# A fused attention and mixture-of-experts kernel: the router's normalisation moved from GpSimd to VectorE, and the third token group's operands made without GpSimd

## The chip, the core and the metric

The kernel runs on one core of a Trainium2 chip. The time is the device time of one execution in microseconds. The engines are TensorE (PE; PEld is its weight load), VectorE (DVE), ScalarE (ACT), GpSimd (POOL) and SyncE (SP), whose queue issues nearly all DMAs.

## What is computed

Linear attention, then a gated feed-forward layer, then a mixture of eight experts with a soft router, on 2304 tokens of width 512. The last part is the one that the change touches:

```python
logits = x @ w_gate
logits = logits - logits.max()
P = np.exp(logits)
for _ in range(8):
    P /= P.sum(1, keepdims=True) + 1e-09
    P /= P.sum(0, keepdims=True) + 1e-09
    P *= N / E
out = np.zeros((N, D), dtype=np.float32)
for e in range(E):
    h = np.maximum(x @ w1[e], 0.0)
    ye = h @ w2[e]
    out += P[:, e:e + 1] * ye
```

Here x has 2304 x 512 elements, E is 8, w1[e] is 512 x 1024 and w2[e] is 1024 x 512.

## The kernel before

Everything is float32, split into a high part in TensorE's reduced format (fp32r) and a low part that is the rest; a product is three matmuls (high x high, low x high, high x low). The order of instructions on each engine is the order in which the program writes them, so a step that stands earlier in the program holds up everything behind it on its engine.

The expert stage works through three token groups of 768 tokens (`GROUPS`), each through 8 experts in 4 units of 256 hidden columns: 32 units (`PER`) per group, numbered 0 to 95. The matrix products use Strassen's scheme: seven products of quarter matrices, M1 to M7. Their right-hand sides are the quarters B11, B12, B21, B22 of x and the sums T1 to T4 of them (T1 = B12 - B11, T2 = B22 - T1, T3 = B22 - B12, T4 = B21 - T2), 2 x 384 columns each. `operands` (from L1107) makes these for a group: `summed` makes a T, `high` copies the high part on ScalarE, `low` subtracts for the low part. It is a generator that does one step of a list per call; in the list, T1 is a sum, hT1 its high part, lT1 its low part, and a G in a step puts it on GpSimd instead of VectorE. Each operand gets a tile of the pool `xs`, which has 8 places.

Units 0 to 31 also prepare the experts' weights: `prep_first` and `prep_second` split a unit's weights into high and low parts (L1042 to L1089 on VectorE), some instructions per call of `prep_tick`, and store them to DRAM (`kept`), from where the units of the later groups read them (`recall`). In such a unit `m2_burst` (L1260) writes the products M2, M6, M5, M7, M4, M3 and calls `mid(k)` between them; the first product of the next unit (`m2_m1`) and four of the six second-layer blocks (`m2_s2`) follow. On VectorE the line L1265 adds two products into `cs` and so frees a PSUM bank, L1211 makes the low half of the hidden layer in `hw` and `hq`.

The router's probabilities, 128 partitions x 18 tiles x 8 experts in the tile `probs`, are normalised by the generator `sinkhorn` (from L919). Its steps are put between the work of units 0 to 6 by `next(steps)`: at `mid(4)` and behind the second-layer blocks 0 and 2 of each unit. First comes the maximum over everything, with GpSimd's `partition_all_reduce` (L924). Then in each of eight iterations GpSimd adds the eight columns in three halving steps (`plus`, L931), VectorE takes the reciprocal `rs` (L942), GpSimd multiplies (`times`, L932), adds the 18 tiles in five steps, sums over the partitions (L950) and scales (L951), VectorE takes the reciprocal `ca` (L955), and GpSimd multiplies again.

In groups 1 and 2 (units 32 to 95) a unit is `m2_p1`, the seven first-layer products of unit n, and `m2_p2`, the second layer of unit n - 1; `work(k)` is called at places in both. L1379 adds two products (`add`), L1335 applies relu and the token's probability (`half_mul`), L1349 makes a low part, L1353 a sum for the second layer, L1446 (`m2_fold`) folds a second-layer product from PSUM into `acc`. The probabilities come back as rows spread over all partitions, by `probs_in`, alternating between two places, `pb_place`. The last unit of a group has a plain second layer, `m2_plain`, whose 18 adds are L1486.

The third group's operands are made in a list `ORDER2` of 18 steps: T1 and T2 from units 62 and 63 on, all sums and the low parts of all T on GpSimd, the rest in units 63 and 64. The tiles `fx` and `fy` hold B11 and B22, B21 and B12 of the hidden layer; `fy` takes the place of `accx`, the output of group 0's last two tiles.

## Time and profile before

| | before |
|---|---|
| median of 3 runs | 2132.41 us (2132.09 to 2135.24) |
| the profiled execution | 2136.45 us |
| its span | 2134.6 us, granted TensorE clock 0.975 on average |
| PE busy | 2009.7 us (94%) |
| DVE busy | 1576.8 us (74%) |
| ACT busy | 804.8 us (38%) |
| POOL busy | 201.3 us (9%) |
| chain that ended last | PE 84%, issue 6%, DVE 4%, POOL 2% |

The profile comes from one execution; its times count from the span's start. The span is what the profiler records; the execution's own time lies 1.85 us above it. Group 0 of the expert stage runs from about 560 to 1175 us, group 1 to about 1653, group 2 to the end. Where an engine is idle, the profile names what ended the wait; "issue" means that nothing it shows did.

### The profile page before, as it was taken

To read this page: it belongs to the slowest core of one execution; us is meant where nothing else is said; L and a number is where in the kernel's file an instruction comes from. 1 tells how busy PE (TensorE), PEld (TensorE's weight loads), DVE (VectorE), ACT (ScalarE), POOL (GpSimd) and SP (SyncE) were. 2 spreads that over 40 slices of the span, in tenths; PEclk is the share of its full clock that TensorE was granted. 3 is DMA by queue.
4 is the path that set the end of the run, shared out by engine and by line. 5 is a ranking of instruction groups with operands and counts; after the bars stand their busy time and mean duration, and the time that the engine had idled before them with its cause. 6 is when DMAs were issued, how large, how long until landed. Compare 5 with 4: busy or idle time off the path is not lost.

```text
span 2134.6 us, 29119 instructions
## 1 busy us (share of the span) xinstructions
PE 2009.7 (94%) x10837; PEld 1867.6 (87%) x10837; DVE 1576.8 (74%) x3107; ACT 804.8 (38%) x1594; POOL 201.3 (9%) x274
## 2 busy tenths in 40 slices
PE   8999999999955569999999999999998999999999
PEld 7788888888844458889998999999998999999999
DVE  7865752535633347877777899999999899999998
ACT  5644531323423235545444333333333333333332
POOL 3532211111112210000000000000003000000000
PEclk9999999999977779999999999999999999999999
DMA  8400320100442448778787777776675777667673
GB/s 258 126 23 24 110 65 1 50 35 1 166 154 106 160 177 311 295 292 301 285 315 301 274 261 253 267 261 252 255 269 198 269 259 257 268 257 253 255 265 119
DMA packets 135493, 429.54 MB, mean 201 GB/s; under 512 B 11816, under 2 KB 68024, under 8 KB 135352
## 3 DMA queue, kind: packets, MB, share of 16 engines
q1 hardware_dynamic: 135080, 427.56, 55.4%
q8 instruction: 85, 1.39, 0.3%
q14 instruction: 56, 0.46, 0.1%
q10 hardware_dynamic: 272, 0.13, 0.0%
HBM read 306.20 MB, written 121.45 MB: 200 GB/s over the span
## 4 chain that ended last, share of the span: by engine, by line
PE 84%; issue 6%; DVE 4%; POOL 2%; ACT 1%; DMA 1%; POOLq 0%; ACTq 0%; DVEq 0%
PE sb L1190 30%; PE sb L1431 12%; PE yb L1431 9%; PE yb L1224 3%; PE yb L1225 3%; PE yb L1223 3%; PE pg L801 2%; PE pv L801 2%; PE y L803 2%; PE pg L802 2%; PE pg L803 2%; PE pv L803 2%; PE pv L802 2%; PE y L802 2%; PE y L801 2%
## 5 line engine op out<-in xcount | busy, mean ns | idle before, releaser
L1446 DVE TENSOR_TENSOR acc<-sb,acc 128x384 f32<-128x384 f32 x480 | 260.8, 558 | 27.0 <-PE sb L1431 23.0
L1190 PE MATMUL sb<-op0T,u 128*128 128x384 f32 x768 | 160.2, 353 | 78.6 <-DVE cs L1265 78.6
L1190 PEld LDWEIGHTS sb<-op0T,u 128*128 128x128 f32 x768 | 145.2, 201 | 86.6 <-DVE cs L1265 81.6
L1190 PE MATMUL sb<-op1T,u 128*128 128x384 f32 x768 | 143.9, 335 | 3.3 <-DVE fx L1379 3.3
L1190 PE MATMUL sb<-op2T,u 128*128 128x384 f32 x768 | 144.7, 336 | 0.8 <-ACT mt L1383 0.5
L1190 PEld LDWEIGHTS sb<-op1T,u 128*128 128x128 f32 x768 | 134.0, 188 | 3.9 <-DVE fx L1379 3.9
L1190 PEld LDWEIGHTS sb<-op2T,u 128*128 128x128 f32 x768 | 133.9, 188 | 2.4 <-DVE fx L1379 1.6
L834 DVE SCALAR_TENSOR_TENSOR th<-th,pg 128x512 f32<-128x512 f32 (+1 forms) x60 | 37.9, 632 | 131.4 <-ACT th L833 131.2
L1190 PE MATMUL sb<-op2B,u 128*128 128x384 f32 x576 | 110.8, 335 | 2.7 <-issue 1.7
L1190 PE MATMUL sb<-op1B,u 128*128 128x384 f32 x576 | 110.5, 335 | 2.4 <-DVE fy L1379 2.2
L1190 PE MATMUL sb<-op0B,u 128*128 128x384 f32 x576 | 111.5, 337 | 0.5 <-ACT pT L1311 0.5
L1379 DVE TENSOR_TENSOR fx<-mt,sb 128x384 f32<-128x384 f32 x128 | 70.9, 554 | 54.4 <-ACT mt L1383 42.3
L1431 PE MATMUL sb<-hc,u 128*128 128x384 f32 x504 | 104.4, 335 | 2.2 <-DVE acc L1446 2.2
L841 POOL TENSOR_TENSOR h<-th,h 128x512 fp32r<-128x512 f32 (+1 forms) x60 | 73.2, 1220 | 339.3 <-ACT h L840 339.3
L1190 PEld LDWEIGHTS sb<-op0B,u 128*128 128x128 f32 x576 | 101.5, 188 | 3.4 <-ACT pT L1311 0.8
L1190 PEld LDWEIGHTS sb<-op2B,u 128*128 128x128 f32 x576 | 100.7, 188 | 3.3 <-issue 2.0
L1190 PEld LDWEIGHTS sb<-op1B,u 128*128 128x128 f32 x576 | 100.6, 188 | 3.2 <-DVE fy L1379 2.6
L1431 PE MATMUL sb<-hd,u 128*128 128x384 f32 x492 | 101.7, 334 | 0.0
L1431 PE MATMUL yb<-hd,u 128*128 128x384 f32 x426 | 96.7, 334 | 0.0
L801 PE MATMUL pg<-x,w 128*128 128x512 f32 (+1 forms) x240 | 90.4, 377 | 1.3 <-ACT x L591 1.3
L803 PE MATMUL y<-h,w 128*128 128x512 f32 (+1 forms) x240 | 89.1, 371 | 2.1 <-POOL w L371 2.1
L1431 PEld LDWEIGHTS sb<-hc,u 128*128 128x128 f32 x504 | 88.8, 188 | 2.5 <-DVE acc L1446 2.5
(330 smaller groups left out, 4915.7 us busy)
## 6 DMA issues: line engine op xcount, KB each, us to landing
u<-kept SPq DMA_DIRECT2D x252, 896.0 KB, 6.2
kept<-u SPq DMA_DIRECT2D x64, 896.0 KB, 5.5
kept<-u SPq DMA_DIRECT2D x62, 768.0 KB, 4.4
rw<-in_moe_w_dram SPq DMA_DIRECT2D x64, 512.0 KB, 5.8
kept<-u SPq DMA_DIRECT2D x62, 128.0 KB, 3.9
raw<-in_moe_w_gate_dram SPq DMA_DIRECT2D x10, 512.0 KB, 3.6
...
```

Source lines behind the costliest of these rows:

```text
L801: nc.tensor.matmul(o, lhsT=w(0), rhs=xb[0], start=first, stop=False)
L802: nc.tensor.matmul(o, lhsT=w(0), rhs=xb[1], start=False, stop=False)
L803: nc.tensor.matmul(o, lhsT=w(1), rhs=xb[0], start=False, stop=last)
L834: nc.vector.scalar_tensor_tensor(out=th[:, 0:n], in0=th[:, 0:n], scalar=1.0, in1=pg[:, 0:n], op0=ALU.add, op1=ALU.mult)
L841: nc.gpsimd.tensor_tensor(out=h[:, 1, 0:n], in0=th[:, 0:n], in1=h[:, 0, 0:n].bitcast(F32), op=ALU.subtract)
L1190: nc.tensor.matmul(bank[:, 0:NT], lhsT=w[wz][:, WI[wname], c, :], rhs=x[:, xz, c, :], start=(start and c == 0 and j == 0), stop=(c == 1 an ...
L1223: nc.tensor.matmul(py, lhsT=h[:, 0, s], rhs=w2[0][:, d], start=(u == 0 and f == 0), stop=False)
L1224: nc.tensor.matmul(py, lhsT=h[:, 0, s], rhs=w2[1][:, d], start=False, stop=False)
L1225: nc.tensor.matmul(py, lhsT=h[:, 1, s], rhs=w2[0][:, d], start=False, stop=(u == UE - 1 and f == 1))
L1379: add = lambda o, a, b: nc.vector.tensor_tensor(out=o, in0=a, in1=b, op=ALU.add)
L1431: nc.tensor.matmul(bank[:, 0:NT], lhsT=w[wz][:, d], rhs=h[:, hz], start=(start and k == 0), stop=True, skip_group_check=True)
L1446: nc.vector.tensor_tensor(out=a, in0=bank[:, 0:NT], in1=a, op=ALU.add)
```

## The change

`sinkhorn` now does its arithmetic on VectorE, three pieces per iteration with a yield ahead of each: sum over the experts, EPS, reciprocal; multiply, sum over the tiles, and GpSimd's `partition_all_reduce`; EPS, reciprocal, and one instruction that multiplies by N/E and by the reciprocals. The steps are also taken at `mid(0)`, so four per unit instead of three. GpSimd keeps the partition sums alone.

`ORDER2` has no G any more. Its first seven steps (T1, hT1, lT1, T2, hT2, lT2, T4) are done in units 40 to 46, one in each, at the end of `m2_p2`; the others in units 63 and 64. No tile of `xs` is taken for group 2: T1 and T2 lie in eight strips of 384 columns at the ends of the tiles of group 1's operands and of `hb`, in two parts of one chunk each, so that `high` and `low` take twice as many instructions for them; the other five operands take the tiles of group 1's operands that are no longer read. The second place of `probs_in` is now the old place of `fy` (tile `pb1`), and `fy` the one in `acc[1]` where the odd probabilities were.

```diff
-        room = tp.tile([P, 512], F32, tag="th", name="room")
...
-        plus = lambda o, x, y: nc.gpsimd.tensor_tensor(out=o, in0=x, in1=y, op=ALU.add)
-        times = lambda w: nc.gpsimd.tensor_tensor(out=probs, in0=probs, in1=w, op=ALU.mult)
         for i in range(ITERS):
-            if i == 0:
-                yield
-            plus(h, probs[:, :, 0:4], probs[:, :, 4:8])
-            plus(h[:, :, 0:2], h[:, :, 0:2], h[:, :, 2:4])
+            yield
             rs = mp.tile([P, NTILE], F32, tag="rs", name=f"rs{i}")
-            plus(rs, h[:, :, 0], h[:, :, 1])
-            nc.gpsimd.tensor_scalar(out=rs, in0=rs, scalar1=EPS, scalar2=None, op0=ALU.add)
+            nc.vector.tensor_reduce(out=rs, in_=probs, axis=AX.X, op=ALU.add)
+            nc.vector.tensor_scalar(out=rs, in0=rs, scalar1=EPS, scalar2=None, op0=ALU.add)
+            nc.vector.reciprocal(out=rs, in_=rs)
             yield
-            nc.vector.reciprocal(out=rs, in_=rs)
-            times(rs.unsqueeze(2).to_broadcast([P, NTILE, E]))
-            plus(c, probs[:, 0:9], probs[:, 9:18])
...
+            nc.vector.tensor_tensor(
+                out=probs, in0=probs, in1=rs.unsqueeze(2).to_broadcast([P, NTILE, E]), op=ALU.mult
+            )
+            cs = mp.tile([P, E], F32, tag="cs", name=f"cs{i}")
+            nc.vector.tensor_reduce(out=cs, in_=probs.rearrange("p t e -> p e t"), axis=AX.X, op=ALU.add)
             ca = mp.tile([P, E], F32, tag="ca", name=f"ca{i}")
-            nc.gpsimd.partition_all_reduce(ca, c[:, 0], P, bass_isa.ReduceOp.add)
-            nc.gpsimd.tensor_scalar(
-                out=ca, in0=ca, scalar1=EPS, scalar2=float(E) / N, op0=ALU.add, op1=ALU.mult
+            nc.gpsimd.partition_all_reduce(ca, cs, P, bass_isa.ReduceOp.add)
+            yield
+            nc.vector.tensor_scalar(out=ca, in0=ca, scalar1=EPS, scalar2=None, op0=ALU.add)
+            nc.vector.reciprocal(out=ca, in_=ca)
+            nc.vector.scalar_tensor_tensor(
+                out=probs,
...
-                if k == 4:
+                if k in (0, 4):
                     next(steps, None)
...
-            pb_place = [halves, [flat[1][:, z * NT : (z + 1) * NT] for z in (3, 4)]]
+            pb_place.append(halves)
...
-    fy = xp.tile([P, 1024], F32, tag="xt0", name="fy")
+    pb1 = xp.tile([P, 1024], F32, tag="xt0", name="pb1")
+    pb_place.append([pb1[:, z * NT : (z + 1) * NT] for z in range(2)])
+    fy = flat[1][:, 3 * NT : 5 * NT]
...
-    ORDER2 = ["TG1", "hT1", "lT1G", "TG2", "hB11", "hT2", "lT2G", "TG4", "lB11", "hB21", "hT4", "lT4G", "TG3"]
-    ORDER2 += ["lB21", "hB22", "hT3", "lT3G", "lB22"]
+    for name, old in (("B11", "B11"), ("B21", "B21"), ("T4", "T2"), ("T3", "T1"), ("B22", "T3")):
+        homes[name] = halves_of(tiles[1, old])
+    room = [t[:, 4 * NT : 5 * NT] for t in [tiles[1, name] for name in IN_RING] + [hb_tile]]
+    for k, name in enumerate(("T1", "T2")):
+        homes[name] = None, [[room[4 * k + 2 * z + c] for c in range(2)] for z in range(2)]
+    ORDER2 = ["T1", "hT1", "lT1", "T2", "hT2", "lT2", "T4", "hB11", "hB21", "hT4", "lB11", "lB21", "hB22", "lT4", "T3"]
+    ORDER2 += ["hT3", "lB22", "lT3"]
...
-        if g == 1 and n % PER == PER - 2:
-            until("TG1")
         if start and g > 1:
-            m2_plain(n - 1, lambda k: until(("hB22", "hB22", "lT3G", "lB22")[k]) if k != 1 else None)
-            m2_p1(n, idle)
+            m2_plain(n - 1, at_k("hB22", None, "lT4", "T3"))
+            m2_p1(n, at_k("hT3", "lB22", None, "lT3"))
...
         elif plain(n) and g == 1:
-            m2_p1(n, lambda k: until("TG2") if k == 1 else None)
-            m2_p2(n - 1, lambda k: until(("hB11", "lB11", "hB21", "lB21")[k]))
+            m2_p1(n, at_k(None, "hB11", "hB21", "hT4"))
+            m2_p2(n - 1, at_k(None, "lB11", None, "lB21"))
         else:
             m2_p1(n, idle, (2, 1, 3, 3) if n == PER + 1 else (2, 1, 0, 2))
-            m2_p2(n - 1, idle)
+            pre = n - PER - 8
+            m2_p2(n - 1, at_k(None, None, None, ORDER2[pre]) if g == 1 and 0 <= pre < 7 else idle)
```

The order on the engines shows three places. The first is GpSimd in the normalisation, from the end of one iteration's tile sums to the next multiplication before the change (an ISA row with tiles is a `partition_all_reduce`; one without tiles stands alone):

```order
L931 TENSOR_TENSOR room<-room 128x8 x2
L950 ISA
L950 ISA ca_5016<-room 128x8
L951 ISA
L951 TENSOR_SCALAR ca_5016<-ca_5016 128x8
L932 TENSOR_TENSOR probs<-probs,ca_5016 128x144
```

and with the change, from the maximum on:

```order
L924 ISA
L924 ISA gma<-gm 128x1
L941 ISA ca_4980<-cs_4978 128x8
L941 ISA ca_5068<-cs_5066 128x8
L941 ISA ca_5202<-cs_5200 128x8
```

The rows without tiles at each sum and behind it are gone; the five other sums follow in the same way, and nothing of GpSimd's stands behind the eighth.

The second is VectorE at the end of unit 3, where the normalisation's fourth iteration is; before the change the unit's end holds one reciprocal between pieces of weight preparation (`t`, `u`; `rw` is the loaded weight):

```order
L1211 SCALAR_TENSOR_TENSOR hw<-cs,hw 128x384
L1056 TENSOR_TENSOR u_0_1_5400<-s_5401,u_0_0_5399 128x512
L1058 TENSOR_TENSOR u_0_1_5400<-s_5401,u_0_0_5399 128x512
L1076 TENSOR_TENSOR t_5487<-rw_1_5283 128x256
L1077 TENSOR_TENSOR t_5487<-t_5487,rw_1_5283 128x256
L1080 TENSOR_TENSOR t_5487<-rw_1_5283 128x256
L1081 TENSOR_TENSOR t_5487<-rw_1_5283,t_5487 128x256
L955 RECIPROCAL ca_5460<-ca_5460 128x8
```

and with the change:

```order
L1227 SCALAR_TENSOR_TENSOR hw<-cs,hw 128x384
L1080 TENSOR_TENSOR u_1_1_5268<-rw_1_5116,u_1_0_5267 128x1024
L1083 TENSOR_TENSOR u_1_1_5268<-t_5266,u_1_0_5267 128x512
L1085 TENSOR_TENSOR u_1_1_5268<-t_5266,u_1_0_5267 128x512
L935 TENSOR_TENSOR probs<-probs,rs_5288 128x144
L939 TENSOR_REDUCE cs_5327<-probs 128x8
L943 TENSOR_SCALAR ca_5329<-ca_5329 128x8
L944 RECIPROCAL ca_5329<-ca_5329 128x8
L945 SCALAR_TENSOR_TENSOR probs<-probs,ca_5329 128x144
L931 TENSOR_REDUCE rs_5364<-probs 128x18
L932 TENSOR_SCALAR rs_5364<-rs_5364 128x18
L1281 TENSOR_TENSOR cs<-mc_5310,sb_4675 128x384
```

The third piece of the iteration (L943) now stands directly behind the second (L939), with nothing between, and ahead of the next unit's first `cs`.

The third is VectorE at the beginning of group 2, from the last adds of `m2_plain` to the first add into `fx`; before:

```order
L1486 TENSOR_TENSOR acc_106<-yb_4827,acc_106 128x384
L1140 TENSOR_TENSOR op2B_13515<-acc_108,op2B_13515 128x2x256
L1140 TENSOR_TENSOR op2B_13515<-acc_108,op2B_13515 128x2x128
L1486 TENSOR_TENSOR acc_105<-yb_4824,acc_105 128x384
L1486 TENSOR_TENSOR acc_105<-yb_4825,acc_105 128x384
L1379 TENSOR_TENSOR fx<-mt_9395,sb_4674 128x384
```

and with the change:

```order
L1150 TENSOR_TENSOR op1T_9276<-acc_107,op1T_9276 128x2x256
L1150 TENSOR_TENSOR op1T_9276<-acc_107,op1T_9276 128x2x128
L1502 TENSOR_TENSOR acc_106<-yb_4827,acc_106 128x384
L1163 TENSOR_TENSOR acc_107<-acc_108 128x2x256
L1163 TENSOR_TENSOR acc_107<-acc_108 128x256
L1502 TENSOR_TENSOR acc_105<-yb_4824,acc_105 128x384
L1502 TENSOR_TENSOR acc_105<-yb_4825,acc_105 128x384
L1150 TENSOR_TENSOR op1T_9302<-acc_108,op1T_9302 128x2x256
L1150 TENSOR_TENSOR op1T_9302<-acc_108,op1T_9302 128x2x128
L1395 TENSOR_TENSOR fx<-mt_9354,sb_4674 128x384
```

lT4 (the first two rows) and T3 (L1163) have come into VectorE's list, and lB22 has moved behind the last two adds, directly ahead of the add into `fx`.

## Rows read from the trace of the kernel before

**Rows 1.** Stretches: us, PE, PEld, DVE, ACT, POOL (x count), PEclk, DMA share, GB/s.

```profile
589.71:793.13 203.42, 111.49 (x470) 98.36 (x469) 72.52 (x151) 50.64 (x99) 42.43 (x100) 0.76 0.40 142
840.41:902.71 62.30, 62.30 (x314) 56.28 (x313) 48.80 (x95) 30.81 (x62) 0.00 (x0) 1.00 0.83 304
...
1200.00:1400.00 200.00, 200.00 (x1155) 200.00 (x1154) 180.97 (x357) 67.59 (x137) 0.00 (x0) 1.00 0.70 256
...
1600.00:1680.00 80.00, 73.06 (x421) 70.92 (x419) 74.23 (x132) 28.65 (x60) 16.80 (x14) 1.00 0.52 188
```

**Rows 2.** Waits, 589.71 to 793.13 us: who for whom, us in total, times, longest.

```profile
DVE ca L955 <- POOL ca L951: 107.0, 8, 16.9
...
DVE cs L1265 <- ACT u L1278: 11.0, 6, 2.3
...
PE sb L1190 <- DVE cs L1265: 77.4, 6, 14.7
...
POOL ca L950 <- issue: 57.5, 8, 8.1
POOL ca L951 <- issue: 56.3, 8, 7.7
```

**Rows 3.** Chain of waits in the first iteration: start us, us, what.

```profile
595.27 7.54 issue
602.81 0.42 POOL ca L950
...
603.32 6.64 issue
```

**Rows 4.** Timeline of DVE, first iteration: start, us, engine, line, operation [idle before].

```profile
592.21 0.26 DVE L942 RECIPROCAL rs<-rs 128x18 f32<-128x18 f32 x1
...
610.18 0.20 DVE L955 RECIPROCAL ca<-ca 128x8 f32<-128x8 f32 x1 [16.12 <-POOL ca L951]
```

**Rows 5.** Timeline at the maximum.

```profile
575.71 0.29 DVE L922 TENSOR_REDUCE gm<-probs 128x1 f32<-128x144 f32 x1
...
575.93 1.21 DVE L1084 TENSOR_TENSOR u<-rw,u 128x1024 fp32r<-128x1024 f32 x1
...
576.14 1.24 POOL L924 PARTITION_ALL_REDUCE gma<-gm  x1 [15.18 <-DVE gm L922]
...
577.66 0.29 DVE L926 TENSOR_SCALAR probs<-probs,gma 128x144 f32<-128x144 f32 x1
```

**Rows 6.** Groups of DVE instructions by line and shape, 570 to 800 us: busy, mean ns.

```profile
L1084 DVE TENSOR_TENSOR u<-rw,u 128x1024 fp32r<-128x1024 f32 x8 | 9.9, 1239 | 0.0
...
L1046 DVE TENSOR_TENSOR s<-rw 128x256 f32<-128x256 f32 x7 | 3.0, 429 | 0.0
...
L922 DVE TENSOR_REDUCE gm<-probs 128x1 f32<-128x144 f32 x1 | 0.3, 293 | 0.0
...
L918 DVE TENSOR_TENSOR probs<-lT,lo 128x16 f32<-128x16 f32 x1 | 0.2, 175 | 0.5 <-ACT lo L917 0.5
```

**Rows 7.** Timeline at the start of group 1.

```profile
1183.91 0.55 DVE L1379 TENSOR_TENSOR fy<-mt,sb 128x384 f32<-128x384 f32 x1 [2.46 <-DMA out_dram<-accx]
...
1184.52 0.79 PE L1190 MATMUL sb<-op1B,u 128*128 128x384 f32 x3 [2.23 <-DVE fy L1379]
```

**Rows 8.** Timeline where groups 1 and 2 meet.

```profile
1628.55 1.65 DVE L1349 TENSOR_TENSOR hc<-acc,hc 128x384 fp32r<-128x384 f32 x1
...
1632.18 1.31 PE L1190 MATMUL sb<-op1T,u 128*128 128x384 f32 x6 [2.23 <-DVE fx L1379]
...
1641.41 1.31 PE L1431 MATMUL sb<-hc,u 128*128 128x384 f32 x6 [2.19 <-DVE acc L1446]
...
1653.30 2.35 PE L1190 MATMUL sb<-op2B,u 128*128 128x384 f32 x12 [1.73 <-issue]
1654.51 1.02 DVE L1140 TENSOR_TENSOR op2B<-acc,op2B 128x512 fp32r<-128x512 f32 x2
```

**Rows 9.** Timeline of DVE in a regular unit of group 1.

```profile
1305.41 0.55 DVE L1379 TENSOR_TENSOR fx<-mt,sb 128x384 f32<-128x384 f32 x1 [0.70 <-ACT mt L1383]
```

More of the change, by code (lines that the diff above doesn't have):

```diff
@@ L954, in sinkhorn @@
-            yield
-            nc.vector.reciprocal(out=ca, in_=ca)
-            times(ca.unsqueeze(1).to_broadcast([P, NTILE, E]))
+            nc.vector.tensor_tensor(
[3 more added lines that the diff above has]
+            nc.vector.tensor_reduce(out=cs, in_=probs.rearrange("p t e -> p e t"), axis=AX.X, op=ALU.add)
+            ca = mp.tile([P, E], F32, tag="ca", name=f"ca{i}")
@@ L1103, in prep_until, with halves_of @@
             prep_tick()
-    X2 = {}
+    X2, tiles, fulls, homes = {}, {}, {}, {}
+    def halves_of(t):
+        full = t[:, 0 : 4 * NT].rearrange("p (z c t) -> p z c t", z=2, c=2)
+        return full, [[full[:, z, c] for c in range(2)] for z in range(2)]
     def operands(g, order, temp, chunk):
@@ L1124, in make @@
         def make(name):
-            t = xs(f"op{g}{name}", F32R)[:, 0 : 4 * NT].rearrange("p (z c t) -> p z c t", z=2, c=2)
-            X2[g][name] = t
-            return t
+            if g == 2:
+                full, at_ = homes[name]
+            else:
+                tiles[g, name] = xs(f"op{g}{name}", F32R)
+                full, at_ = halves_of(tiles[g, name])
+            X2[g][name] = at_
+            fulls[g, name] = full
+            return at_
         def at(w, s):
@@ L1133, in high @@
             t = make(name)
+            full = fulls[g, name]
             for s, x in T[name] if name in T else B[name]:
-                nc.scalar.copy(out=t[:, 0, :, s], in_=x)
+                if full is not None:
+                    nc.scalar.copy(out=full[:, 0, :, s], in_=x)
+                else:
+                    for c in range(2):
+                        nc.scalar.copy(out=t[0][c][:, s], in_=x[:, c])
         def low(name, eng):
-            t = X2[g][name]
+            t, full = X2[g][name], fulls[g, name]
+            sub = lambda o, x, h: eng.tensor_tensor(out=o, in0=x, in1=h.bitcast(F32), op=ALU.subtract)
             for s, x in T[name] if name in T else B[name]:
-                eng.tensor_tensor(out=t[:, 1, :, s], in0=x, in1=t[:, 0, :, s].bitcast(F32), op=ALU.subtract)
+                if full is not None:
+                    sub(full[:, 1, :, s], x, full[:, 0, :, s])
+                else:
+                    for c in range(2):
+                        sub(t[1][c][:, s], x[:, c], t[0][c][:, s])
         def summed(name, eng):
@@ L1780, in temp2 @@
         ]
-    ORDER2 = ["TG1", "hT1", "lT1G", "TG2", "hB11", "hT2", "lT2G", "TG4", "lB11", "hB21", "hT4", "lT4G", "TG3"]
-    ORDER2 += ["lB21", "hB22", "hT3", "lT3G", "lB22"]
+    for name, old in (("B11", "B11"), ("B21", "B21"), ("T4", "T2"), ("T3", "T1"), ("B22", "T3")):
[5 more added lines that the diff above has]
+    ORDER2 += ["hT3", "lB22", "lT3"]
     later = operands(2, ORDER2, temp2, None)
     until = lambda step: next(x for x in later if x == step)
+    at_k = lambda *steps: lambda k: until(steps[k]) if k < len(steps) and steps[k] else None
     idle = lambda k: None
```

20 lines of the change are left out of this document (10 added, 10 removed).

## The prediction

> **What bounds the kernel now.** I read the busy time by stretches first [rows 1]. In a steady stretch of token group 0 (840 to 903 us) TensorE is busy 62.30 of 62.30 us at clock 1.00, with VectorE at 48.8; in group 1 it is busy 200 of 200 with VectorE at 181. So TensorE is the bound, and another engine costs time only where TensorE waits for it. Two stretches are different. In 589.71 to 793.13 us TensorE is busy 111.5 of 203.4 us and its granted clock is 0.76 on average, between its two levels; this is where the router normalisation runs. In 1600 to 1680 us, where group 1 ends and group 2 begins, it is busy 73.06 of 80.
>
> Next the sum of waits in the first stretch [rows 2]. VectorE stood 107.0 us in front of eight reciprocals `ca` (L955) waiting for GpSimd's L951, and TensorE 77.4 us for VectorE's `cs`, whose instruction is queued behind that reciprocal. GpSimd stood 57.5 us before its eight partition sums and 56.3 us before the eight L951 that follow them, both times on "issue", so on nothing that another engine did. The chain of waits puts these on the path [rows 3]: 7.54 us of issue, a sum of 0.42 us, 6.64 us of issue. On VectorE one iteration is then 592.21 to 610.18 us, `rs` to `ca`, with 16.12 us of idle time [rows 4]. In GpSimd's list of instructions a bare ISA row without tiles stands just where each issue time is: before each sum, and behind it before the next ordinary operation. I take that row to be a switch of GpSimd's code.
>
> What the stretch should cost comes from the steady one: 470 matmuls ran in it, and 314 take 62.30 us there [rows 1], so 470 x 62.30 / 314 = 93.3 us. The excess is 203.4 - 93.3 = **110.1 us**: the waits, and the matmuls that ran at the lower clock after each of them.
>
> **The change part by part.**
>
> *Partition sums.* After the change GpSimd's list holds one bare ISA row, ahead of the maximum (L924), then eight sums with nothing between. All sixteen issue times should go. What stays is a round trip VectorE to GpSimd and back. The maximum is the nearest row: the reduction starts at 575.71, GpSimd's part at 576.14 takes 1.24 us, and VectorE goes on with the result at 577.66 [rows 5], so from the reduction's end (576.00) at most 1.66 us. I take 1.66 for a sum. Upper end: 7.54 + 0.42 + 6.64, about 15 [rows 3], if the issue time belongs to the sum itself. I take the low end because the maximum, with its switch done in advance, shows no such time behind it on VectorE.
>
> *The normalisation's arithmetic on VectorE.* Per iteration six small instructions come (both reciprocals were there before): two reductions over 144 elements at 0.293 us like the maximum's; two TENSOR_SCALARs on 18 and 8 elements, 0.20 us like the reciprocal on 8 [rows 4]; two products on 144 elements, between 0.175 for 16 and 0.429 for 256, in proportion 0.31 [rows 6]. That is 0.59 + 0.40 + 0.62 = 1.6 us, 12.8 us for eight. The reduction over every eighth element might cost twice as much, 2.3 us more in all. VectorE was busy 72.5 us in the stretch; 72.5 + 12.8 = 85.3 of 93.3 us still fits.
>
> *Waits that are added.* The piece behind a sum now waits on VectorE for GpSimd. VectorE's order tells what lies between (weight preparation, 0.43 us for 256 elements [rows 6] and in proportion): in the fourth iteration nothing, in the third 1.1 us, in the seventh 1.5, in the eighth 1.7; in the others 4.5 us or more. Waits of VectorE: 1.66 + 0.56 + 0.16, some 2.4 us. Behind them is queued the `cs` that frees a PSUM bank; at the fourth iteration TensorE has most of the four second-layer blocks of the unit before it needs that bank, so it hides. The pieces that go into the middle of a burst push the low half of `hq`, which the second layer waits for, back by 0.6 to 0.75 us; no row shows its slack alone. I take 0.5 us per unit for six units, **+3**, near the low end, since TensorE never waits in the steady stretch with VectorE at 78%. Bounds: nothing, and all of the new work plus eight whole round trips on the path, 12.8 + 2.3 + 13.3 = 28.
>
> *Places of fy and of the odd probabilities.* At the start of group 1 the add into `fy` waited 2.46 us for the store from `accx`, whose place it takes, and TensorE 2.23 us for that add [rows 7]. `fy` moves to a free place; the load of probabilities takes the old one on SP's queue. It may stand there about as long, with weight loads behind it that are two units early. **-2.2** (0 at worst).
>
> *T1, T2 and T4 in group 1.* Five VectorE steps enter units 40 to 46, one per unit, behind the last fold. T1, T2 and T4 take 1.02 us like the pair of 512 and 256 elements [rows 8]; the two low halves, in four instructions, 1.2 us between the rows for 256 and 16. Behind the last fold VectorE has 0.70 us of idle time [rows 9]; so 0.3 or 0.5 us each shows at TensorE, less what its bank order hides: **+1.5** (0 to 5). The ScalarE copies go into gaps and cost nothing with ScalarE at 67.6 of 200 us [rows 1].
>
> *Boundary of groups 1 and 2.* GpSimd's operations made VectorE slow: 1.65 us for a low half of 384 elements [rows 8] against 0.55 [rows 9]. Half of GpSimd's 16.8 us there [rows 1], some 8 us, I put down as VectorE's loss. TensorE's waits there, 2.23, 2.19 and 1.73 us [rows 8], follow from it, and 80 - 73.06 = 6.9 us is lost in all [rows 1]. After the change VectorE gives back the 8 us but takes lT4, T3 and lT3, 3 x 1.02 us. They stand late: when TensorE ends the plain product, VectorE still has about T3 (1.02), two adds (1.0), lB22 (1.02) and, with its rest of other adds (1.0), the add of 0.55 that frees the bank for M5, 4.6 us in all; M1, M2 and M6 last some 3.1 (two took 2.35 [rows 8], the overhang of the last matmul included). So M5 waits about 1.5 us; for M7's low half I add 0.4, for lB11 and lB21 in unit 63 0.5, and 0.5 for the rest. So 6.9 becomes about 2.9: **-4** (-6.9 to 0).
>
> The sum: -110.1 + 3 - 2.2 + 1.5 - 4 = -111.8. The profiled execution took 2136.45 us (span 2134.6), so 2024.7 for one like it. The median of the three runs, 2132.41, is 4.0 below; on that scale the forecast is **2021 us**.
>
> *A rule against it.* GpSimd's maximum ran beside a 128x1024 subtraction on VectorE, which took 1.21 us [rows 5] where eight of them average 1.24 [rows 6]: no sign that the two blocked each other. The Trainium skill's page SBUF — State Buffer, section SBUF: two separate sides, says that VectorE and GpSimd share a port pair as an exclusive lock, and that the loser "fully blocks" for the whole instruction when VectorE has two SBUF inputs. By it each sum would hold VectorE up by its own length, an estimate of 8 x 1.24 = 9.9 us on VectorE, and 85.3 + 9.9 would pass 93.3. The slow low halves at the boundary agree with the rule, the maximum's neighbour doesn't.
>
> **The rivals.**
>
> *VectorE becomes the bound of the normalisation's units.* It needs reductions at twice their price, or sums and VectorE instructions that hold each other up. For it: 91% of VectorE's time is spoken for. Against it: the maximum's neighbour [rows 5]. With 12.8 + 2.3 of work, 9.9 of holding up and 2.4 of waits, VectorE needs 72.5 + 27.4 = 99.9 us, plus the 11.0 for which it waits on ScalarE's copies [rows 2]: 110 in place of 93.3 + 3, so **2035 us**. The port rule above would end here.
>
> *The switch happens all the same.* Then each sum keeps 15 us. Between sum and use lie 4.5, 8, 1.1, 0, 4.7, 8, 1.5 and 1.7 us, 29.5 in all, so VectorE waits 8 x 15 - 29.5 = 90.5 us, 16.5 less than now, and its 12.8 us of new work stand beside no TensorE work that is ready: 2132.4 - 16.5 + 12.8 + 3 - 4.7 (the three last terms of the sum), **2127 us**. Against it: the rows are gone from the list.
>
> *Slower.* One mechanism: a sum beside a busy VectorE takes so long that the third piece waits more than the old reciprocal did. At 18 us, the whole of the old iteration from `rs` to `ca` [rows 4], the waits are 8 x 18 - 29.5 = 114.5 us, 7.5 more than now: 2132.4 + 7.5 + 12.8 + 3 - 4.7 = **2151 us**. It decides from a round trip of 15.7 us, where these terms cancel. The maximum shows 1.66, beside a busy VectorE.
>
> **How the numbers follow.** The forecast has 0.88, VectorE as bound 0.07, the switch that stays 0.03, slower 0.02. No change, within 0.2% (4 us, about what a measurement of this kernel can tell), lies between the last two and has 0.01 of their chance; faster 0.97, slower 0.02. The low end takes the good bounds, no delay in the normalisation, none in units 40 to 46 and none at the boundary: 2021 - 3 - 1.5 - 2.9 = 2013.6, less the 1 to 2 us by which runs differ: 2012. The high end takes in VectorE as bound with its dear end, 28 us on the path in place of 3: 2046.
>
> **What would show it.** Right: GpSimd's only issue time of 7 us left is at the maximum; TensorE's clock is 1.00 through the normalisation, and its six units take 94 to 100 us; VectorE's waits for GpSimd add up to a few us, the longest in the fourth iteration; no TensorE wait of 2 us where `fy` is first written; some 3 us lost between 1490 and 1570 us where groups 1 and 2 meet, VectorE's low halves there at 0.55; one short TensorE wait in units 40 to 46. Wrong: issue time before each sum, sums over 2 us, or TensorE waits for VectorE in every unit of the normalisation.

## The result and the profile after

The changed kernel takes 2019.95 us (median of 4 runs, 2018.83 to 2021.36) against 2132.25 (4 runs, 2131.62 to 2135.24): ratio 0.9471, 95% interval 0.9455 to 0.9487, 112.3 us less. The forecast was 2021. The profiled execution took 2018.83 us, its span 2017.0.

The page: busy time, the granted clock over the span, one queue that loads instructions, the chain that ended last.

```profile
PE 1989.9 (99%) x10837; PEld 1849.4 (92%) x10837; DVE 1585.0 (79%) x3175; ACT 806.1 (40%) x1598; POOL 143.7 (7%) x162
...
PEclk9999999999999999999999999999999999999999
...
q8 instruction: 85, 1.39, 0.3%
...
PE 91%; DVE 4%; ACT 1%; issue 1%; POOL 1%; DMA 1%; ACTq 0%; DVEq 0%
```

TensorE is busy 99% of the span, the granted clock is 0.9 or more in every slice and 0.999 on average, so at its upper level, and 5 of the 6% of issue have left the chain.

Two stretches: the same six units of the normalisation as the first of [rows 1], from the same kind of copy to the same kind of copy, and the boundary of groups 1 and 2, the last of [rows 1].

```profile
587.08:682.45 95.37, 94.76 (x470) 83.92 (x469) 80.52 (x194) 50.72 (x98) 4.30 (x7) 1.00 0.84 303
...
1486.00:1566.00 80.00, 77.09 (x444) 74.87 (x443) 72.00 (x144) 28.20 (x60) 0.00 (x0) 1.00 0.60 213
```

The same 470 matmuls take 95.37 us instead of 203.42, at clock 1.00 instead of 0.76. At the boundary 2.9 us of TensorE are lost instead of 6.9.

The waits of 587 to 683 us, against [rows 2]:

```profile
POOL ca L941 <- DVE cs L939: 80.8, 7, 13.9
...
DVE ca L943 <- POOL ca L941: 0.8, 2, 0.5
...
PE sb L1206 <- DVE cs L1281: 0.6, 2, 0.3
```

VectorE's 107.0 us in front of GpSimd have become 0.8, TensorE's 77.4 us in front of `cs` 0.6. GpSimd has no issue time there; it waits for VectorE. (The first of the eight sums lies just ahead of this stretch.) Its timeline, with the maximum and four of the eight sums:

```profile
573.52 1.24 POOL L924 PARTITION_ALL_REDUCE gma<-gm  x1 [15.21 <-DVE gm L922]
585.65 0.44 POOL L941 PARTITION_ALL_REDUCE ca<-cs  x1 [10.89 <-DVE cs L939]
...
608.84 0.77 POOL L941 PARTITION_ALL_REDUCE ca<-cs  x1 [13.87 <-DVE cs L939]
622.59 0.40 POOL L941 PARTITION_ALL_REDUCE ca<-cs  x1 [12.97 <-DVE cs L939]
...
656.23 1.44 POOL L941 PARTITION_ALL_REDUCE ca<-cs  x1 [13.41 <-DVE cs L939]
```

VectorE around the fourth and the seventh sum; the fourth is the one behind which nothing else lies:

```profile
622.07 0.42 DVE L939 TENSOR_REDUCE cs<-probs 128x8 f32<-128x144 f32 x1
623.02 0.17 DVE L943 TENSOR_SCALAR ca<-ca 128x8 f32<-128x8 f32 x1 [0.53 <-POOL ca L941]
...
656.02 0.45 DVE L1042 TENSOR_TENSOR s<-rw 128x256 f32<-128x256 f32 x1
656.35 0.45 DVE L1043 TENSOR_TENSOR s<-rw,s 128x256 f32<-128x256 f32 x1
656.69 0.71 DVE L1046 TENSOR_TENSOR u<-rw,u 128x512 fp32r<-128x512 f32 x1
657.70 0.17 DVE L943 TENSOR_SCALAR ca<-ca 128x8 f32<-128x8 f32 x1 [0.30 <-POOL ca L941]
```

The round trip is 0.53 us bare (622.49 to 623.02) and 1.56 at its longest (656.14 to 657.70). The new instructions, groups by line and shape: busy, mean ns, idle before.

```profile
L939 DVE TENSOR_REDUCE cs<-probs 128x8 f32<-128x144 f32 x8 | 3.5, 441 | 0.3
...
L945 DVE SCALAR_TENSOR_TENSOR probs<-probs,ca 128x144 f32<-128x144 f32 x8 | 2.5, 308 | 0.3
L935 DVE TENSOR_TENSOR probs<-probs,rs 128x144 f32<-128x144 f32 x8 | 2.4, 303 | 0.0
...
L931 DVE TENSOR_REDUCE rs<-probs 128x18 f32<-128x144 f32 x8 | 2.4, 297 | 0.0
...
L932 DVE TENSOR_SCALAR rs<-rs 128x18 f32<-128x18 f32 x8 | 1.4, 176 | 0.3
...
L943 DVE TENSOR_SCALAR ca<-ca 128x8 f32<-128x8 f32 x8 | 1.3, 168 | 0.8 <-POOL ca L941 0.8
```

Together 13.5 us. TensorE's waits at the boundary, in its timeline, against the last of [rows 8]:

```profile
1525.25 1.33 PE L1447 MATMUL sb<-hc,u 128*128 128x384 f32 x6 [0.44 <-DVE acc L1462]
...
1538.91 0.98 PE L1206 MATMUL sb<-op1B,u 128*128 128x384 f32 x4 [0.36 <-DVE fx L1395]
...
1548.95 0.97 PE L1206 MATMUL sb<-op1T,u 128*128 128x384 f32 x4 [0.54 <-ACT mt L1399]
...
1564.11 2.00 PE L1206 MATMUL sb<-op1B,u 128*128 128x384 f32 x10 [1.46 <-DMA u<-kept]
```

In groups 1 and 2 a unit's length is the time from its first copy on ScalarE (L1399, before L1383) to the next unit's; a regular unit has 14.57 us. Lengths in us in the profiled executions of the kernels (what their names mean stands in the next section):

| unit | before | after | normalisation only | operands only | late, VectorE | late, GpSimd | early, GpSimd | last three on GpSimd | old place of fy |
|---|---|---|---|---|---|---|---|---|---|
| 32 | 9.90 | 7.37 | 8.90 | 7.37 | 7.37 | 7.36 | 7.37 | 7.37 | 9.06 |
| 42 | 14.57 | 14.57 | 14.56 | 14.59 | 14.57 | 14.56 | 16.39 | 14.57 | 14.57 |
| 45 | 14.57 | 14.58 | 14.57 | 14.56 | 14.58 | 14.58 | 16.40 | 14.57 | 14.57 |
| 41, 43, 46, 47 | 58.26 | 58.92 | 58.27 | 59.25 | 58.27 | 58.29 | 58.34 | 58.97 | 58.93 |
| 62 to 65 | 71.82 | 66.83 | 73.23 | 66.04 | 71.51 | 71.47 | 66.04 | 66.94 | 66.84 |

What the parts gave, from the two profiled executions: normalisation 203.42 to 95.37, -108.05; unit 32, -2.53; units 41, 43, 46 and 47, +0.66; units 62 to 65, -4.99: together -114.9. The spans differ by 117.6; 2.6 of that lies ahead of the normalisation (589.71 against 587.08), where the change does nothing, so it is a difference between two runs; the two kernels below with an ordinary operation beside the sum, alike up to that point, lie 2.2 us apart at the maximum. Before's profiled execution lies 4.2 us above its median, after's 1.1 below: 117.6 - 4.2 - 1.1 = 112.3.

### The profile page after: what moved, and what is told of

Same layout as the page of the kernel before. It is cut to its first block, busy times and chain, and to the rows that moved or that the text cites. A ratio compares the mean times of both kernels' runs of the same rounds, so it can differ in the third digit from the quotient of the medians.

```text
span 2017.0 us, 29032 instructions
## 1 busy us (share of the span) xinstructions
PE 1989.9 (99%) x10837; PEld 1849.4 (92%) x10837; DVE 1585.0 (79%) x3175; ACT 806.1 (40%) x1598; POOL 143.7 (7%) x162
## 3 DMA queue, kind: packets, MB, share of 16 engines
q8 instruction: 85, 1.39, 0.3%
## 4 chain that ended last, share of the span: by engine, by line
PE 91%; DVE 4%; ACT 1%; issue 1%; POOL 1%; DMA 1%; ACTq 0%; DVEq 0%
PE sb L1206 34%; PE sb L1447 12%; PE yb L1447 9%; PE yb L1241 4%; PE yb L1240 4%; PE yb L1239 4%; PE pv L801 2%; PE pg L801 2%; PE pv L803 2%; PE pv L802 2%; PE pg L803 2%; PE pg L802 2%; PE y L801 2%; PE y L803 2%; PE y L802 2%
## 5 line engine op out<-in xcount | busy, mean ns | idle before, releaser
L1206 PE MATMUL sb<-op1T,u 128*128 128x384 f32 x1536 | 299.3, 335 | 1.6 <-DVE fx L1395 1.0
L1206 PEld LDWEIGHTS sb<-op1T,u 128*128 128x128 f32 x1536 | 269.0, 188 | 4.0 <-DVE fx L1395 2.6
L1206 PE MATMUL sb<-op1B,u 128*128 128x384 f32 x1120 | 220.8, 335 | 2.1 <-DMA u<-kept 1.5
L1206 PEld LDWEIGHTS sb<-op1B,u 128*128 128x128 f32 x1120 | 196.1, 188 | 3.7 <-DMA u<-kept 1.8
L1206 PE MATMUL sb<-op0T,u 128*128 128x384 f32 x768 | 149.3, 335 | 1.8 <-DVE cs L1281 1.8
L1206 PEld LDWEIGHTS sb<-op0T,u 128*128 128x128 f32 x768 | 135.5, 188 | 8.8 <-DVE cs L1281 3.5
L801 PE MATMUL pg<-x,w 128*128 128x512 f32 (+1 forms) x240 | 90.1, 375 | 1.3 <-ACT x L591 1.3
L803 PE MATMUL y<-h,w 128*128 128x512 f32 (+1 forms) x240 | 88.5, 369 | 2.1 <-POOL w L371 2.1
L801 PE MATMUL y<-h,w 128*128 128x512 f32 (+1 forms) x240 | 89.9, 374 | 0.0
L801 PE MATMUL pv<-x,w 128*128 128x512 f32 (+1 forms) x240 | 89.5, 373 | 0.0
L802 PE MATMUL pg<-x,w 128*128 128x512 f32 (+1 forms) x240 | 88.7, 370 | 0.6 <-DVE x L592 0.6
L803 PE MATMUL pv<-x,w 128*128 128x512 f32 (+1 forms) x240 | 88.6, 369 | 0.0
```

Source lines behind the costliest of these rows:

```text
L801: nc.tensor.matmul(o, lhsT=w(0), rhs=xb[0], start=first, stop=False)
L802: nc.tensor.matmul(o, lhsT=w(0), rhs=xb[1], start=False, stop=False)
L803: nc.tensor.matmul(o, lhsT=w(1), rhs=xb[0], start=False, stop=last)
L1206: nc.tensor.matmul(bank[:, 0:NT], lhsT=w[wz][:, WI[wname], c, :], rhs=x[xz][c], start=(start and c == 0 and j == 0), stop=(c == 1 and j == 2),
```

## The experiments

The theory after the result: the 110 us were GpSimd's switches between two kinds of instruction, its own operations and the partition sum; where the arithmetic is done matters little; the second part of the change gives some 6 us more. The rivals: GpSimd's arithmetic itself was the price; the parts lean on each other; the pieces' places, not the switches, keep TensorE running. Each run was compared with the kernel before on the same chip, so ratios are compared: after has 0.9471, and one thousandth is 2.1 us. Half-widths of the intervals are 0.0014 to 0.002, so 4 to 5 us between two of them is the least that times alone tell apart; below that the unit lengths and the waits decide.

**The two halves apart.** First the kernel before with only the new `sinkhorn` and the second call per unit:

```diff
-                if k == 4:
+                if k in (0, 4):
```

> The kernel before with the new normalisation alone (three pieces per iteration on VectorE, GpSimd with the sums only, and the second call per unit); places of fy, T1, T2, T4 and group 2's operands as before. Theory (the prediction's terms): the normalisation gives 110.1 - 3 = 107 us and the rest of the change 4.7, so about 2132 - 107 = 2025 us (2022 to 2029), and the six units of the normalisation last 95 to 96 us. Rival (the parts lean on each other, for instance group 2's operands gain only because GpSimd's switch is gone): above 2030 or below 2020 us.

Then the changed kernel with the old `sinkhorn` put back:

```diff
-                if k in (0, 4):
+                if k == 4:
```

> The changed kernel with the old normalisation put back: fy's new place, the five steps in group 1 and the boundary without GpSimd stay. Theory: the second part alone gives 2.5 (fy) + 5.0 (boundary) - 1.3 (steps in group 1) = 6.2 us, as the unit times of the changed kernel's profile have it: about 2126 us (2124 to 2129). Rival (half of what the boundary shows is the normalisation's doing or chance): 2130 to 2133 us.

Measured: 2027.2 us, ratio 0.9495 (0.9481 to 0.9509), and 2127.38, ratio 0.9958 (0.9941 to 0.9975), against 2134.95 of the kernel before there: -107.8 and -7.6, both as the theory had them. Their sum, 115.3, is after's 5.3% within the intervals, so the halves add up. One thing did lean on the other: unit 32 lasts 8.90 us with the new normalisation alone, 9.90 before. Units 62 to 65 last 73.23 us there, 1.4 more than before; no run shows why.

**An ordinary operation beside the sum.** One operation on 128 x 8 elements goes to GpSimd, eight times, behind the sum

```diff
             nc.gpsimd.partition_all_reduce(ca, cs, P, bass_isa.ReduceOp.add)
+            nc.gpsimd.tensor_scalar(out=ca, in0=ca, scalar1=EPS, scalar2=None, op0=ALU.add)
             yield
-            nc.vector.tensor_scalar(out=ca, in0=ca, scalar1=EPS, scalar2=None, op0=ALU.add)
```

> The changed kernel, but the EPS is added to each partition sum by GpSimd, an ordinary operation on 128 x 8 elements right behind the sum, and not by VectorE: one instruction of 0.2 us moved, eight times. Theory (the time goes to GpSimd's switch between the sums and ordinary operations): an issue time of about 7 us stands behind each sum before the add; it hides where 4.5 us or more of VectorE's work lie between, so VectorE waits some 8 x 7.5 - 29.5 = 30 to 37 us and TensorE loses 25 to 45: 2045 to 2065 us. The issue time before each sum comes back too (7 us), but the next sum's data is 10 us or more away, so part of it hides. Rival (GpSimd's time was that of the arithmetic it did, some 1 us per operation): 8 x 1 us of it, at most 2020 to 2024 us.

or ahead of it:

```diff
+            nc.gpsimd.tensor_scalar(out=cs, in0=cs, scalar1=EPS, scalar2=None, op0=ALU.add)
             nc.gpsimd.partition_all_reduce(ca, cs, P, bass_isa.ReduceOp.add)
```

> The changed kernel, but GpSimd adds EPS to its input right ahead of each sum (the partition partials get 1e-9 more each, which changes nothing that counts): one ordinary operation on 128 x 8 more per iteration, ahead of the sum instead of behind it. Theory (switch): the add itself needs a switch back that can run while GpSimd waits for its data, the sum's switch of about 7 us cannot, since it is issued behind the add: 7.5 us more between the third piece's reduction and the sum, VectorE waits 30 to 37 us in all, 2045 to 2065 us, about as for the operation behind the sum. Rival (arithmetic only): 2020 to 2024 us. If only one direction costs, one of these two runs comes out near 2020 and the other doesn't.

Measured: 2072.93 us, ratio 0.9709 (0.9690 to 0.9729), and 2061.59, ratio 0.9656 (0.9637 to 0.9675): 51 and 40 us over after, for eight operations of 0.27 us. The arithmetic rival falls. GpSimd's timeline with the operation behind the sum:

```profile
587.76 0.43 POOL L941 PARTITION_ALL_REDUCE ca<-cs  x1 [10.89 <-DVE cs L939]
595.65 0.26 POOL L942 TENSOR_SCALAR ca<-ca 128x8 f32<-128x8 f32 x1 [7.45 <-issue]
601.71 0.59 POOL L941 PARTITION_ALL_REDUCE ca<-cs  x1 [5.79 <-DVE u L1049]
```

and ahead of it:

```profile
585.59 0.27 POOL L941 TENSOR_SCALAR cs<-cs 128x8 f32<-128x8 f32 x1 [10.89 <-DVE cs L939]
591.91 0.43 POOL L942 PARTITION_ALL_REDUCE ca<-cs  x1 [6.05 <-issue]
599.30 0.52 POOL L941 TENSOR_SCALAR cs<-cs 128x8 f32<-128x8 f32 x1 [6.96 <-DVE hw L1228]
```

Both directions cost; in each kernel it is mainly the switch that stands behind the data that shows. The other runs while GpSimd waits for VectorE anyway: in six of eight places GpSimd goes on as soon as VectorE's data is there, in the other two 1.0 to 2.1 us later (here the sum at 601.71, whose data was ready at 600.61). In the list of the waits these are 62.8 us (8 times, up to 9.9) behind the sum and 52.5 (up to 7.7) ahead of it; VectorE waits 42.5 and 34.9. The second is inside the 30 to 37 expected; the first is outside, as is its time, since the switch after a sum took 7.85 us on average where 7.5 were put down, and TensorE's waits went up to 8.2 us, behind which it ran at the lower clock (mean 0.86 from 580 to 735 us). The instructions of one line, in the first of the two kernels, show what stands at a switch (durations in ns):

```profile
L942 POOLq MODIFY_POOL_CONFIG  x16: 108/108/108, 588.1 to 713.3; - x16
```

Two of these per switch, at the sequencer, 108 ns each; the other 7 us have no row. So the switch is shown. That it loads code is what the names say, not what the trace shows: the instruction queue q8 has the same 85 packets and 1.39 MB in all kernels, the second one, q14, 55 to 57 packets. The Trainium skill, page GPSIMD Engine Reference, section 2.1 Instruction dispatch, says that the first call to newly loaded GpSimd code pays about 6 us, 5.95 measured, with no visible instruction. The kernel with the operation ahead of the sum agrees, with 5.95 to 6.05 us in four of its first five switches; its others took up to 7.68, and those behind the sum 6.89 to 9.88.

**The arithmetic on GpSimd, the sum on TensorE.** GpSimd does the small operations as before, in three pieces; only the partition sum leaves it, as a product with a 128 x 128 tile of ones:

```diff
+            plus(c[:, 0], c[:, 0], c[:, 8])
+            yield
+            total = sbank[(0, 1, 1, 0)[i % 4]][:, 384 : 384 + E]
+            nc.tensor.matmul(total, lhsT=ones, rhs=c[:, 0], start=False, stop=True, skip_group_check=True)
...
-            nc.gpsimd.partition_all_reduce(ca, cs, P, bass_isa.ReduceOp.add)
```

> The changed kernel, but GpSimd does the normalisation's arithmetic again as in the kernel before (some nine small operations per iteration), in three pieces per iteration, and the sums over the partitions are made by TensorE (128 x 128 ones times 128 x 8, into spare columns of a PSUM bank, whose old contents may be added in), so that no GpSimd instruction of another kind stands between the ordinary ones. Theory (the 110 us were the switch, not the place of the arithmetic): no issue time on GpSimd, and the time is near the changed kernel's, 2022 to 2032 us, the rest for waits of a few tenths of a microsecond at the eight extra products. Rival (GpSimd is too slow for the chain, or holds VectorE up at the SBUF): 2060 to 2100 us.

Measured: 2028.99 us, ratio 0.9504 (0.9485 to 0.9523), in the theory's range, 6.6 us over after though GpSimd is busy 35 us there. Its waits, 580 to 720 us:

```profile
POOL room L933 <- issue: 7.0, 1, 7.0
PE sb L952 <- POOL room L933: 5.1, 4, 1.8
```

One switch, after the maximum. TensorE now waits for GpSimd at its extra products: 5.1 us. So of the 107 us some 100 come back without VectorE doing the arithmetic, by taking the switches away.

**One piece per iteration.** The first kernel has each iteration with its sum in one piece, two iterations per unit at the tails; the second moves only the cut, so that the same work stands at the same tails but the sum's round trip lies between two pieces:

```diff
-                if k in (0, 4):
-                    next(steps, None)
...
+        yield
         for i in range(ITERS):
-            yield
...
             nc.gpsimd.partition_all_reduce(ca, cs, P, bass_isa.ReduceOp.add)
+            yield
```

(The first has the yield at the head of the loop and none elsewhere.)

> The changed kernel, but each iteration is one piece on VectorE, with the sum's round trip inside it, two iterations per unit at the tails of the first and third second-layer block and none in the middle of the burst. Theory (the pieces only hide the round trip, 0.53 us each where it was seen bare): VectorE waits 8 x 0.53 = 4.2 us more, TensorE hides nearly all of it: 2020 to 2024 us. Rival (the pieces are what keeps TensorE running: 3 us of new work in a row plus the wait holds up the copies that free its banks): 2030 to 2040 us.

> The kernel with one piece per iteration, but the cut lies right behind the sum and not ahead of the iteration: a piece is the rest of the last iteration and this one up to its sum, the same 2.2 us of VectorE's work at the same two tails per unit, while the sum's round trip now lies between two pieces. Theory A (the 12 us that one piece per iteration lost are the waits of 0.5 us for the sum, 4.2 us in all, which delay the add that frees TensorE's bank): 2020 to 2024 us, and TensorE's waits for that add are gone. Theory B (they come from putting 4.4 us of work in a row ahead of that add at the tails, with no steps in the burst): 2029 to 2034 us, and VectorE's waits for the sum are gone while TensorE still waits 2 to 3 us per unit.

Measured: 2034.2 us, ratio 0.9529 (0.9514 to 0.9544), 12 over after: my theory fell, the rival held. Then 2026.53, ratio 0.9488 (0.9472 to 0.9504), between the two theories' ranges. Waits of the first, 580 to 720 us:

```profile
PE sb L1204 <- DVE cs L1279: 10.8, 4, 3.9
...
DVE ca L941 <- POOL ca L940: 4.2, 8, 0.6
```

of the second, 575 to 720 us:

```profile
PE sb L1205 <- DVE cs L1280: 6.6, 4, 2.9
...
DVE ca L942 <- POOL ca L940: 0.5, 1, 0.5
```

Taking 3.7 us of waits for the sum off VectorE took 4.2 off TensorE's, so at this place they were on the path. The other 6.6 us I put down to the normalisation's work in front of `cs`, which frees a bank; after's four places per unit leave 0.6. By time the second kernel lies only 3 to 4 us over after, less than times alone tell apart. The first also lost time to the clock. TensorE's timeline of the first,

```profile
598.94 4.21 PE L1204 MATMUL sb<-op0T,u 128*128 128x384 f32 x12 [3.38 <-DVE cs L1279]
...
620.18 3.18 PE L1204 MATMUL sb<-op0T,u 128*128 128x384 f32 x12 [2.90 <-DVE cs L1279]
```

and of the second:

```profile
649.52 2.35 PE L1205 MATMUL sb<-op0T,u 128*128 128x384 f32 x12 [2.92 <-DVE cs L1280]
```

In the first kernel twelve matmuls took 4.21 us behind a wait of 3.38 (the granted clock there is 0.50, its lower level) and 3.18 behind one of 2.90 (0.69 on average); in the second they took 2.35 behind one of 2.92, at 1.00. Waits of the same length were followed by different clocks, so no single wait decides.

**fy back in its old place.**

```diff
-    pb1 = xp.tile([P, 1024], F32, tag="xt0", name="pb1")
-    pb_place.append([pb1[:, z * NT : (z + 1) * NT] for z in range(2)])
-    fy = flat[1][:, 3 * NT : 5 * NT]
+    fy = xp.tile([P, 1024], F32, tag="xt0", name="fy")
+    pb_place.append([flat[1][:, z * NT : (z + 1) * NT] for z in (3, 4)])
```

> The changed kernel with fy and the odd probabilities back in their old places. Theory: the add into fy waits for the store from accx again, some 2.2 to 2.5 us at TensorE in the first unit of group 1, whose length goes from 7.4 back to 9.9 us: 2022.5 us. Rival (the wait went with the normalisation's earlier end, not with the place): no change, 2020 us.

Measured: 2020.53 us, ratio 0.9465 (0.9446 to 0.9484); the time tells nothing. The trace does: the wait is back (waits, 1040 to 1110 us),

```profile
DVE fy L1395 <- DMA out_dram<-accx: 1.6, 1, 1.6
...
PE sb L1206 <- DVE fy L1395: 1.4, 1, 1.4
```

and unit 32 has 9.06 us instead of 7.37. So the place is worth 1.7 us beside the new normalisation, where the add waits 1.6 us in the old place, and 2.5 beside the old, where it waited 2.46 [rows 7].

**The boundary.** Three of its steps go back to GpSimd:

```diff
-    ... "lB11", "lB21", "hB22", "lT4", "T3"]
-    ORDER2 += ["hT3", "lB22", "lT3"]
+    ... "lB11", "lB21", "hB22", "lT4G", "TG3"]
+    ORDER2 += ["hT3", "lB22", "lT3G"]
```

> The changed kernel, but T3 and the low halves of T4 and T3 at the boundary of groups 1 and 2 are made by GpSimd again (three steps of 768 elements). Theory of the prediction (GpSimd's operations slow VectorE's down): VectorE's low halves and adds there stretch from 0.55 to 1.1 to 1.65 us while GpSimd works, and units 63 and 64 are 1 to 3 us longer: 2021 to 2023 us. Rival (VectorE is loaded too much there and GpSimd would take load off it): 0.5 to 2 us shorter, 2018 to 2019.5 us.

Measured: 2020.45 us, ratio 0.9463 (0.9447 to 0.9479), and units 62 to 65 in 66.94 us against 66.83: neither. Its timeline of GpSimd and VectorE:

```profile
1519.35 2.30 POOL L1150 TENSOR_TENSOR op1T<-acc,op1T 128x512 fp32r<-128x512 f32 x2 [846.56 <-DVE fx L1395]
...
1519.39 1.67 DVE L1351 SCALAR_TENSOR_TENSOR fx<-fx,pb 128x384 f32<-128x384 f32 x1
...
1540.52 1.14 DVE L1351 SCALAR_TENSOR_TENSOR fx<-fx,pb 128x384 f32<-128x384 f32 x1
```

The slowing is there, 1.67 and 1.14 us for what takes 0.56 alone, but VectorE is spared three steps of 1.03 us, and at TensorE nothing is left of either. So these three steps on GpSimd were not what cost the boundary its 5 us, as the prediction had it. What else changed there is that five steps left for units 40 to 46. They were put back, once on VectorE and once (with G) on GpSimd, in the places of the kernel before:

```diff
-    ORDER2 = ["T1", "hT1", "lT1", "T2", "hT2", "lT2", "T4", "hB11", "hB21", ...
+    ORDER2 = ["T1", "hT1", "lT1", "T2", "hB11", "hT2", "lT2", "T4", "lB11", "hB21", ...
...
+        if g == 1 and n % PER == PER - 2:
+            until("T1")
...
-            m2_p2(n - 1, at_k(None, None, None, ORDER2[pre]) if g == 1 and 0 <= pre < 7 else idle)
+            m2_p2(n - 1, idle)
```

> The changed kernel, but T1, T2, T4 and the low halves of T1 and T2 are not made in units 40 to 46: they stand where they stood before the change, in the last two units of group 1, still on VectorE. Theory (the boundary's 5 us came from making these steps earlier, since VectorE has no room there: 75 of 84 us): VectorE's 5.4 us more show there, units 62 to 65 together 4 to 6 us longer than the changed kernel's, and units 41 to 49 are 1.3 us shorter: 2022 to 2025 us. Rival (the prediction's view: the loss at the boundary was GpSimd's slowing of VectorE, so with GpSimd away VectorE takes these steps with little loss): units 62 to 65 at most 2 us longer, 2019 to 2021 us.

> The same kernel with the five late steps on GpSimd, as before the change; the later three (T3, low halves of T4 and T3) stay on VectorE. Theory (place in time decides, not the engine): units 62 to 65 longer by 3 to 6 us than the changed kernel's, as with the steps on VectorE to within 1.5 us: 2022 to 2025 us. Rival (GpSimd's slowing of VectorE): 2 us or more longer than with the steps on VectorE.

Measured: 2024.89 us, ratio 0.949 (0.9471 to 0.9509), and 2023.33, ratio 0.9483 (0.9464 to 0.9502). Units 62 to 65 last 71.51 and 71.47 us: 4.7 and 4.6 more than after's, whichever engine does the steps. TensorE's timeline, on VectorE,

```profile
1518.22 2.38 PE L1206 MATMUL sb<-op1T,u 128*128 128x384 f32 x12 [1.45 <-DVE fx L1395]
...
1530.88 1.36 PE L1447 MATMUL sb<-hc,u 128*128 128x384 f32 x6 [2.45 <-DVE acc L1462]
```

and on GpSimd:

```profile
1521.52 2.25 PE L1206 MATMUL sb<-op1T,u 128*128 128x384 f32 x6 [2.15 <-DVE fx L1395]
...
1531.92 1.33 PE L1447 MATMUL sb<-hc,u 128*128 128x384 f32 x6 [1.80 <-DVE acc L1462]
```

In both kernels TensorE waits for VectorE at an add into `fx` (not the same one) and at a fold, together 3.9 and 3.95 us. So for these five steps the place in time decides, and the engine hardly. VectorE's rows beside GpSimd in the second kernel, for example

```profile
1518.36 1.64 DVE L1365 TENSOR_TENSOR hc<-mt,hc 128x384 fp32r<-128x384 f32 x1
```

where 0.55 is usual, are some 4.1 us longer in sum from 1515 to 1532 us, where VectorE spends 5.0 us on the same steps in the first: GpSimd takes little load off VectorE. Unit 65 blurs the figures, since TensorE waits there for a weight load, 1.43 and 1.11 us. Units 63 and 64 alone last 35.48 us in the changed kernel, 40.11 and 40.79 in these two and 41.29 before, so of 5.8 us there 4.6 are the place and at most 1.2 GpSimd.

**The early steps on GpSimd.** If VectorE's five steps lengthen units 41 to 47, an idle GpSimd might do them for nothing:

```diff
-    ORDER2 = ["T1", "hT1", "lT1", "T2", "hT2", "lT2", "T4", ...
+    ORDER2 = ["TG1", "hT1", "lT1G", "TG2", "hT2", "lT2G", "TG4", ...
```

> The changed kernel, but the early steps T1, T2, T4 and the low halves of T1 and T2 are made by GpSimd in the same units 40 to 46. Theory (VectorE's 5.4 us are what lengthens units 41 to 49 by 1.3 us; GpSimd is idle there and VectorE has 1.4 us of room per unit for the slowing): these units return to 14.57 us, 1.3 us less in all, 2018.5 to 2019 us and the shortest of all kernels here. Rival (GpSimd stretches VectorE's instruction beside it by 1.1 us, as one of 0.56 us took 1.67 at the boundary): units 41 to 49 together 0 to 3 us longer than the changed kernel's: 2020 to 2023 us.

Measured: 2021.83 us, ratio 0.9479 (0.9463 to 0.9495). Units 41, 43, 46 and 47 are regular again, but 42 and 45 have 16.39 and 16.40 us. TensorE's timeline there:

```profile
1207.85 2.36 PE L1206 MATMUL sb<-op1T,u 128*128 128x384 f32 x12 [0.26 <-DVE fx L1395]
...
1212.24 1.34 PE L1206 MATMUL sb<-op1T,u 128*128 128x384 f32 x6 [0.99 <-DVE fx L1395]
```

The rival held: 1.8 us in each of the two units where GpSimd works (low half and next sum together), 3.6 against 0.66 on VectorE. No version here beats the changed kernel by what can be told.

## Why the prediction was right, point by point

*Bound and excess.* The steady stretch gave the right yardstick: 93.3 us for 470 matmuls, 95.37 measured, nothing left of the lower clock.

*Partition sums.* The issue times were the switch, and all sixteen went. The round trip was taken at 1.66 us from the maximum; it is 0.53 bare. The maximum was the nearest row but itself takes 1.24 us where a sum takes 0.40, so the term was mis-sized on the safe side; why the maximum takes longer stands under the port rule. VectorE waits 0.8 us, not 2.4, in the fourth iteration, as named, and the seventh. The sign "GpSimd's only issue time of 7 us left is at the maximum" did not come: the maximum stood 15.21 us waiting for VectorE, and its switch ran in that time.

*Arithmetic on VectorE.* 12.8 us put down, 13.5 measured; the reduction over every eighth element costs 1.5 times its neighbour (441 ns), between the once and twice of the bounds. VectorE is busy 80.5 of 95.4 us, not 85.3, though 1.2 us of the new work lie just ahead of that stretch, with the first sum.

*Delay.* +3 assumed, +2.1 measured (95.37 - 93.3). But "near the low end, since TensorE never waits in the steady stretch" was a thinner reason than it looked: with the work at two places per unit instead of four the same work cost 6.6 us of waits, with the round trips inside 10.8. The four places are part of the result.

*fy.* -2.2 predicted, -2.53 measured, and the wait that was named is gone. Beside the new normalisation the place alone is worth 1.7 of it, and the new normalisation alone takes 1.0 us off the unit, so the two overlap.

*T1, T2, T4 in group 1.* +1.5 predicted, some +0.8 measured: the two low halves 0.23 each, T1 and T4 0.09. T2's unit, 44, is not in the table: it has 14.89 us, but the kernel with these steps late has 14.88 there too, and a unit of 14.88 turns up at different places in different kernels. Where it falls elsewhere, unit 44 has 14.67 to 14.69, so T2 costs 0.1. So more of it is hidden at TensorE than was taken; by what, no run shows.

*Boundary.* -4 predicted, -5.0 measured, and here the reasoning failed: the step "GpSimd's operations made VectorE slow ... Half of GpSimd's 16.8 us there, some 8 us, I put down as VectorE's loss" named the wrong cause. The slowing is real, but GpSimd's three steps cost nothing on balance and the five late steps cost 4.7 us on VectorE as on GpSimd. The gain is their move to units 40 to 46, so that the sum came out near was in part luck. The 2.9 us that remain are right in sum and wrong in parts: M5 waits 0.36 us, not 1.5, and 1.46 are a wait for a weight load from DRAM, 0.97 before.

*The port rule.* The rows bear the rule out, and the prediction misread the maximum. It looked at VectorE's subtraction, which began 0.21 us earlier than the maximum and lost nothing; GpSimd was the one held up. In the second kernel with one piece per iteration a sum met the same subtraction:

```profile
643.37 1.21 DVE L1079 TENSOR_TENSOR u<-rw,u 128x1024 fp32r<-128x1024 f32 x1
643.54 1.30 POOL L940 PARTITION_ALL_REDUCE ca<-cs  x1 [12.83 <-DVE cs L938]
```

It took 1.30 us, where a sum with nothing beside it takes 0.40, and ended 0.26 us behind the subtraction; the maximum ended 0.24 behind its own [rows 5], and the seventh sum (1.44 us) 0.27 behind the last of the three weight preparations beside it. Those took 0.45, 0.45 and 0.71 where 0.41, 0.42 and 0.69 are usual. At the boundary GpSimd began first (1519.35 against 1519.39), and VectorE took 1.67 for 0.56; GpSimd's first instruction there took 1.29. The Trainium skill's page SBUF — State Buffer, section SBUF: two separate sides, says that, when VectorE has two inputs in SBUF, whichever of the two engines starts first has the shared ports for its whole instruction and the other one fully blocks; these rows agree. So the 1.24 us taken as a sum's price were mostly a wait for VectorE. That the sums would hold VectorE up did not come, since VectorE's instruction had begun first beside each sum that was lengthened; the time went to GpSimd, off the path.

*The rivals.* VectorE never became the bound; the switch does return with an ordinary GpSimd operation beside the sums (40 and 51 us), so that rival's mechanism is real, but not in this kernel.
